# Attention and soft mixture of experts on one core: new order of all engines, new banks, second buffers for part of the transposed probabilities

## The chip, the cores and the metric

The kernel runs on one core of one Trainium2 chip. The time is the device time of one launch in microseconds (us), the median of the runs shown. TensorE does the matrix products and the transposes into PSUM, VectorE (DVE), ScalarE (ACT) and GpSimd (POOL) the rest, and SyncE (SP) issues the transfers between main memory and SBUF.

## The reference

q, k and v have 8 batches x 8 heads x 576 rows x 64 columns. The attention is masked by blocks of 64: a row sees its own block and those before it. Its output, 4608 rows of 512, goes through a soft mixture of experts with 8 experts of 4 slots each.

```python
scores = scale * np.matmul(q, k.transpose(0, 1, 3, 2))
scores = np.where(mask, scores, -1000000000.0)      # mask: block_i >= block_j
attn = softmax(scores, axis=-1)                     # with + 1e-09 under the sum
x = (attn @ v).transpose(0, 2, 1, 3).reshape(4608, 512)
logits = x @ phi                                    # 512 x 32 slots
d = softmax(logits, axis=0)                         # over all 4608 rows
slot_input = (d.T @ x).reshape(8, 4, 512)
slot_out[e] = np.maximum(slot_input[e] @ w1[e], 0.0) @ w2[e]   # w1: 512x1024, w2: 1024x512
out = softmax(logits, axis=1) @ slot_out            # 4608 x 512
```

## The kernel before

Heads are taken two by two: a pair m (0 to 31, four to a batch) holds one head in partitions 0 to 63 and one in 64 to 127. The nine blocks of 64 rows are grouped by how many key blocks they see. For each pair TensorE does these steps, under the names of the table `TM`:

- UA, UB, UC: the products q k. UA (`qk` with "7") gives the scores of the rows that see up to 512 columns, UB (`qkb`) those with 576 ("8") and the short ones ("3", "2", "1", "0"), UC (`qk` with "5") those with 384.
- g7, gc, gd, g5 (`tr`, line 501): the transposes of the normalized probabilities, 16, 10, 12 and 12 of them, into a pair of PSUM banks (`ptb`).
- pv0 and pv1 (`pv`, line 539) and pa (`pv8`, line 549): the products with v, which give the columns of x.

Between them VectorE takes the row maxima (rm, line 454) and the reciprocals of the sums (z, line 470), ScalarE the exponentials (ex, line 464), GpSimd normalizes (nm, line 481), adds epsilon (ze, line 474) and scales k (ks, line 373). The copies out of PSUM (eg7, og7, ..., for the two banks "e" and "o" of each group of transposes, xa and xb for the output of pa and pv) are done by ScalarE (line 339) or VectorE (line 341), as the table `EN` says.

For each batch the mixture of experts adds: prt0 to prt4 (logits, lines 568 and 579), their statistics (stats, stats1, stats2, lines 596 to 621) and `keep_l` (lines 626 and 627), which keeps the logits for the second softmax; ndt, the transposition of the exponentials; xq0, xq1 and xn4 (`xnat`, line 682), x transposed back, with copies en; sl and sl4, the products that collect the slots; sacc and sacc4, which add them up on VectorE. After the last batch mg0 to mg6 merge the running maxima, `formed` (line 730) builds the slots' input siT, and the experts follow: up (line 948), down (line 968), and the combination with the second softmax. `combine` for the first four batches ("comb0", "comb1") and `turn_c(0)`, a VectorE transposition, prepare that softmax.

The order of every engine is fixed by hand: each step is entered with `at(m * T + TM[...], ...)`, with T = 9.2, the steps are sorted by that number, and each engine runs its own in that order. Keys with ".0" to ".3" are for pair m mod 4, A to D for pairs 0 to 3, w and y for pairs 30 and 31, v and z for the last two batches. Below, "g7.23" is step g7 of pair 23, "xq1#6" step xq1 of batch 6.

Of SBUF, one big tile `arena` holds q, k, v, the probabilities and the transposed probabilities pt0 and pt1 (one buffer for each head); the areas that become free at the end take pieces of the experts' weights, 1 MB each. k is loaded into `kr` and scaled into `ks0` or `ks1` in turns. At the very start eight `warm` matmuls on zeros run before the first data, and two groups of `fill` matmuls later.

Of the kernel before, what the change touches and what calls it, by code (L numbers as in the profile page):

```python
# [29 lines left out]
PT1, PT8, PTN = 896, 1280, 1600  # L30
# [8 lines left out]
ONE = "82"  # L39
# [6 lines left out]
for name, n in (  # L46
    *((f"x{i}", S) for i in XIN), ("kr", S), ("q0", S), ("ks0", S), ("p7_0_0", 512), ("p7_1_0", 512),
    ("p5_0_0", 384), ("p5_1_0", 384),
    ("p3_0", 256), ("p1_0", 128), ("p0_0", 128), ("q1", S), ("ks1", S), ("p8", 640), ("v0", 640),
    ("p3_1", 256), ("p2", 256), ("p1_1", 128), ("p0_1", 128),  # L50
    *((f"p{t}_{j}_1", 64 * t + 64) for t in (7, 5) for j in range(2)),
    ("v1", 640), ("pt0", PTN), ("pt1", PTN), ("phi", 128),
):
    AREAS[name] = (LATE0, LATE0 + n)
    LATE0 += n
# [11 lines left out]
    "T": 9.2, "lkA": -5.94771, "lqA": -2.81305, "lkB": -10.95031, "lqB": -8.91013, "ksA": 2.22677, "UAA":  # L67
    2.24077, "rm71A": 2.24477, "rm70A": 2.24877, "ex71A": 2.25277, "ex70A": 2.25677, "lkC": -15.5701, "UBA":
    5.41282, "rm3A": 5.41482, "rm2A": 5.41682, "rm0A": 5.41882, "rm1A": 5.42082, "ex3A": 5.42282, "ex0A":
    5.42482, "ex1A": 5.42682, "ex2A": 5.42882, "lvB": 0.16944, "UCA": 10.43497, "lqC": -7.96303, "ksB": 4.13543,  # L70
# [134 lines left out]
def tile_attention_softmoe(  # L205
# [81 lines left out]
    with ExitStack() as c1:  # L287
# [15 lines left out]
        def endz(b):  # L303
            return "z" * (b == NB - 1)
# [738 lines left out]
```

## Time and profile before

| | us |
|---|---|
| median of 3 runs | 364.29 |
| range of the runs | 363.56 to 366.44 |
| profiled execution | 365.06 |
| its span, first to last instruction | 363.2 |
| TensorE busy | 347.2 (96%) |
| VectorE busy | 269.2 (74%) |
| ScalarE busy | 268.3 (74%) |
| GpSimd busy | 206.5 (57%) |

The profile is of one execution; times in it count from the first instruction. The attention fills the span to about 303 us, the rebuilding of the last batch to 311.6 us, the experts and the combination the rest. A matmul's busy time includes what it waits in the pipeline behind the one before it.

### The profile page before, as it was taken

Reading aid. Unit: us, or ns where it says so; the run is one execution under the profiler, and the core shown is the slowest. Engines: PE = TensorE matmul, PEld = TensorE weight load, DVE = VectorE, ACT = ScalarE, POOL = GpSimd, SP = SyncE. Lnnn points to the kernel's source line nnn. Section 1 sums busy time; section 2 is a strip of 40 time slices with the busy share of each in tenths; the row PEclk is TensorE's granted clock in tenths of the full one; section 3 lists DMA queues with packets and bytes.
Section 4 is the critical chain, followed back from the end, with each engine's and each line's share of the span. In section 5 each row is a group of like instructions: output and inputs, shape, how many; then the busy total and the mean of one; then the engine's idle time right before and its main releaser. Section 6 shows DMA issues by size and latency. Waiting matters only on the chain.

```text
span 363.2 us, 14376 instructions
## 1 busy us (share of the span) xinstructions
PE 347.2 (96%) x5724; PEld 237.3 (65%) x5724; DVE 269.2 (74%) x756; ACT 268.3 (74%) x855; POOL 206.5 (57%) x472
## 2 busy tenths in 40 slices
PE   8899999999999999999999999999999999999983
PEld 3666666777667766776777676767676766446641
DVE  4877767978897888778877887788778866463442
ACT  3877889887978798889888988898888776022341
POOL 3886577757766776676666666666667573000000
PEclk9999999999999999999999999999999999999995
DMA  6656363654473546453854473627413069999886
GB/s 202 213 192 210 99 175 139 222 168 143 139 279 116 167 147 212 131 189 88 255 189 133 154 240 111 208 68 248 128 45 119 19 229 378 389 423 422 346 347 279
DMA packets 29218, 72.29 MB, mean 199 GB/s; under 512 B 6880, under 2 KB 15200, under 8 KB 24160
## 3 DMA queue, kind: packets, MB, share of 16 engines
q1 hardware_dynamic: 29152, 71.38, 57.2%
q8 instruction: 45, 0.74, 0.8%
q14 instruction: 21, 0.17, 0.1%
HBM read 61.93 MB, written 9.44 MB: 196 GB/s over the span
## 4 chain that ended last, share of the span: by engine, by line
PE 60%; DVE 6%; ACT 1%; issue 1%; POOL 1%; DVEq 0%; ACTq 0%; POOLq 0%
PE x L539 13%; PE sc L412 10%; PE pt_e L501 9%; PE sc L433 5%; PE so L968 4%; PE x L549 4%; PE hp L948 4%; PE o L925 3%; DVE stat L454 2%; PE pt_o L501 2%; PE x L568 2%; DVE arena L341 2%; PE x L702 1%; PE x L682 1%; PE x L579 1%
## 5 line engine op out<-in xcount | busy, mean ns | idle before, releaser
L481 POOL TENSOR_SCALAR arena<-arena,stat 128x512 f32<-128x512 f32 (+6 forms) x288 | 153.1, 548 | 56.2 <-DVE stat L470 38.2
L464 ACT ACTIVATE arena<-sc,stat 128x512 f32<-128x512 f32 (+6 forms) x282 | 150.8, 547 | 9.1 <-DVE stat L454 7.7
L454 DVE TENSOR_REDUCE stat<-sc 128x1 f32<-128x512 f32 (+4 forms) x251 | 130.0, 545 | 8.4 <-PE sc L433 5.5
L501 PEld LDWEIGHTS pt_e<-ident,arena 64*128 64x128 f32 x789 | 60.9, 138 | 35.9 <-POOL arena L481 12.3
L501 PE MATMUL pt_e<-ident,arena 64*128 64x64 f32 x789 | 75.2, 229 | 5.4 <-DVE arena L341 2.3
L539 PE MATMUL x<-arena 128*64 128x128 f32 (+2 forms) x640 | 76.1, 384 | 0.2
L501 PE MATMUL pt_o<-ident,arena 64*128 64x64 f32 x789 | 74.8, 229 | 0.2
L412 PE MATMUL sc<-arena 64*128 64x512 f32 (+1 forms) x252 | 63.2, 583 | 0.2
L501 PEld LDWEIGHTS pt_o<-ident,arena 64*128 64x128 f32 x789 | 59.7, 138 | 3.2 <-ACT arena L339 2.1
L539 PEld LDWEIGHTS x<-arena 128*64 128x64 f32 x640 | 41.1, 136 | 30.2 <-issue 18.2
L464 ACT ACTIVATION_READ_ACCUMULATOR arena<-sc,stat 128x1 f32 x282 | 58.5, 208 | 0.0
L339 ACT COPY arena<-pt_o 128x384 f32<-128x384 f32 (+1 forms) x87 | 44.4, 511 | 16.5 <-PE pt_o L501 13.2
L341 DVE COPY arena<-pt_e 128x384 f32<-128x384 f32 (+2 forms) x72 | 40.9, 568 | 10.2 <-PE x L539 7.4
L433 PE MATMUL sc<-arena 64*64 64x192 f32 (+2 forms) x752 | 43.3, 341 | 0.3 <-ACT arena L464 0.3
L433 PEld LDWEIGHTS sc<-arena 64*64 64x64 f32 x752 | 36.2, 133 | 8.6 <-issue 3.2
L339 ACT COPY arena<-pt_e 128x384 f32<-128x384 f32 (+2 forms) x54 | 26.8, 495 | 16.6 <-PE pt_o L501 13.7
L474 POOL TENSOR_SCALAR stat<-stat 128x2 f32<-128x2 f32 (+1 forms) x96 | 18.9, 197 | 31.2 <-ACT arena L464 26.1
L470 DVE RECIPROCAL stat<-stat 128x2 f32<-128x2 f32 (+1 forms) x96 | 15.5, 167 | 24.7 <-POOL stat L474 23.7
L549 PE MATMUL x<-arena 128*64 128x64 f32 x640 | 25.7, 227 | 0.0
L373 POOL TENSOR_SCALAR arena<-arena 128x576 f32<-128x576 f32 x32 | 21.6, 675 | 6.1 <-DMA arena<-in_k 4.7
L549 PEld LDWEIGHTS x<-arena 128*64 128x64 f32 x640 | 21.3, 137 | 5.6 <-ACT xn L339 3.3
L341 DVE COPY arena<-pt_o 128x384 f32<-128x384 f32 (+2 forms) x39 | 20.6, 529 | 3.8 <-PE pt_o L501 1.7
(166 smaller groups left out, 362.2 us busy)
## 6 DMA issues: line engine op xcount, KB each, us to landing
arena<-in_w SPq DMA_DIRECT2D x32, 1024.0 KB, 7.2
arena<-in_k SPq DMA_DIRECT2D x32, 288.0 KB, 3.2
arena<-in_q SPq DMA_DIRECT2D x32, 288.0 KB, 3.1
arena<-in_v SPq DMA_DIRECT2D x32, 256.0 KB, 3.2
out<-arena SPq DMA_DIRECT2D x7, 1024.0 KB, 5.8
arena<-in_v SPq DMA_DIRECT2D x32, 32.0 KB, 3.1
out<-arena SPq DMA_DIRECT2D x2, 512.0 KB, 4.8
out<-arena SPq DMA_DIRECT2D x4, 256.0 KB, 3.9
```

The lines of the kernel that those rows point to most:

```text
L339: nc.scalar.copy(out=out, in_=in_)
L341: nc.vector.tensor_copy(out=out, in_=in_)
L373: nc.gpsimd.tensor_scalar(out=area(f"ks{m % NQB}"), in0=area("kr" if m > 1 else f"ks{m}"), scalar1=SCALE, scalar2=0.0, op0=ALU.mult, op1=A ...
L412: nc.tensor.matmul(scores(t + str(j), m), lhsT=q[r, lo:lo + 128], rhs=k[r, 0:NC[t]], start=True, stop=True)
L433: nc.tensor.matmul(o, lhsT=a, rhs=b, start=True, stop=True)
L454: nc.vector.tensor_reduce(out=st[:, 0, u:u + n], in_=sc, axis=AX.XY if x == "8" else AX.X, op=ALU.max, negate=True)
L464: nc.scalar.activation(out=pr, in_=sc, func=AF.Exp, bias=st[:, 0, u:u + 1], accum_out=st[:, 1, u:u + 1],)
L474: nc.gpsimd.tensor_scalar(out=st[:, 2, c], in0=st[:, 1, c], scalar1=EPS, scalar2=1.0, op0=ALU.add, op1=ALU.mult)
L481: nc.gpsimd.tensor_scalar(out=pr, in0=pr, scalar1=st[:, 2, u:u + 1], scalar2=0.0, op0=ALU.mult, op1=ALU.add)
L501: nc.tensor.transpose(out=trbank(m, g)[i][:, 64 * n:64 * n + 64], in_=prob(m, x)[r, 128 * c:128 * c + 128], identity=ident[r, r],)
L539: nc.tensor.matmul(xps[m, 0][64 * j:64 * j + 64, lo:hi], lhsT=vs(m)[:, j, c, :], rhs=rhs, start=a, stop=z, skip_group_check=True,)
L549: nc.tensor.matmul(xps[m, 1][64 * j:64 * j + 64, 0:64], lhsT=vs(m)[:, j, c, :], rhs=arena[:, lo:lo + 64], start=(c == 0), stop=(c == NQ - 1),)
```

## The change

k is loaded straight into `ks0` or `ks1` and scaled there. The transposed probabilities of g7 and g5 that pv reads now have two buffers, pa0 and pa1, used in turns; those of gd (pb) and gc (pc) have one. For that the probabilities "3", "0" and "5" have one buffer instead of two. PSUM is cut into four pairs of banks, and a table `BK` names the pair or bank of every step. Bank pair 3 has most transposes as before, but pair 0 puts gc and g5 into bank pair 0, pair 2 puts g5 there. `TM` and `EN` have new numbers for all steps. In the last batch several steps are split in two: the copy xb, part4, the statistics, the transposition ndt, the copies dn, xnat (three pairs, then the fourth), slots, and `formed`, whose halves are copied by ScalarE and by VectorE. `turn_c(0)` stands behind the first "turn" of the experts instead of ahead of them, and the first half of "comb0" and "comb1", comb0, stands in pair 24 instead of pair 31.

```diff
-ONE = "82"
+ONE = ("8", "2", "3", "0", "50", "51")
...
-    *((f"x{i}", S) for i in XIN), ("kr", S), ("q0", S), ("ks0", S), ("p7_0_0", 512), ("p7_1_0", 512),
-    ("p5_0_0", 384), ("p5_1_0", 384),
-    ("p3_0", 256), ("p1_0", 128), ("p0_0", 128), ("q1", S), ("ks1", S), ("p8", 640), ("v0", 640),
-    ("p3_1", 256), ("p2", 256), ("p1_1", 128), ("p0_1", 128),
-    *((f"p{t}_{j}_1", 64 * t + 64) for t in (7, 5) for j in range(2)),
-    ("v1", 640), ("pt0", PTN), ("pt1", PTN), ("phi", 128),
+    *((f"x{i}", S) for i in XIN), ("q0", S), ("ks0", S), ("p7_0_0", 512), ("p7_1_0", 512), ("p1_0", 128), ("v0", 640), ("pa0", PTA), ("q1", S), ("ks1", S), ("p8", 640), ("p3", 256), ("p2", 256), ("p1_1", 128), ("p0", 128),
+    ("p7_0_1", 512), ("p5_0", 384), ("p5_1", 384), ("p7_1_1", 512), ("pa1", PTA), ("v1", 640), ("pb", 2 * PTB), ("pc", 2 * PTC),
...
+BK = {
+    "S7.0": 1, "SB.0": 1, "S8.0": 2, "S5.0": 2, "Tg7.0": 3, "Tg5.0": 3, "Tgc.0": 3, "Tgd.0": 3, "PB.0": 0, "PA.0":
...
+    "PB.3": 0, "PA.3": 0, "S7A": 1, "SBA": 3, "S8A": 2, "S5A": 0, "Tg7A": 3, "Tg5A": 0, "TgcA": 0, "TgdA": 3, "PBA":
...
+    1, "PAA": 0, "S7B": 1, "SBB": 1, "S8B": 2, "S5B": 2, "Tg7B": 3, "Tg5B": 3, "TgcB": 3, "TgdB": 3, "PBB": 0,
+    "PAB": 0, "S7C": 1, "SBC": 1, "S8C": 2, "S5C": 2, "Tg7C": 3, "Tg5C": 0, "TgcC": 3, "TgdC": 3, "PBC": 1, "PAC":
...
-        xbk = [ps.tile([128, 512], F32, name=f"x{i}") for i in range(2)]
-
-
-
-        scm = [ps.tile([128, 512], F32, name=f"sc{j}") for j in range(2)]
-        scn = ps.tile([128, 1024], F32, name="sc8")
-
-        ptb = [ps.tile([128, 512], F32, name=f"pt_{x}") for x in "eo"]
-
-        def xbank(key, z=""):
-            return xbk[EN["X" + key + z]]
+        duo = [
+            ps.tile([128, 1024], F32, name=f"duo{i}") if i in WIDE else [ps.tile([128, 512], F32, name=f"one{i}{j}") for j in range(2)]
+            for i in range(4)
+        ]
...
+        def bank(key, z):
+            return BK.get(key + z, BK.get(key))
...
-            nc.sync.dma_start(out=area("kr" if m > 1 else f"ks{m}"), in_=kT[b, p])
+            nc.sync.dma_start(out=area(f"ks{m % NQB}"), in_=kT[b, p])
...
-                out=area(f"ks{m % NQB}"), in0=area("kr" if m > 1 else f"ks{m}"), scalar1=SCALE, scalar2=0.0, op0=ALU.mult, op1=ALU.add
+                out=area(f"ks{m % NQB}"), in0=area(f"ks{m % NQB}"), scalar1=SCALE, scalar2=0.0, op0=ALU.mult, op1=ALU.add
...
-            return scm if m == NB * NP - 1 and g in ("gc", "g5") else ptb
+            return two(bank("T" + g, sfx(m)))
...
-                dst = both[:, i, PT8:PTN]
+                dst = area("pc").rearrange("p (j c) -> p j c", j=2)[:, i]
             elif g == "gd":
-                dst = both[:, 1 - i, PT1:PT8]
+                dst = area("pb").rearrange("p (j c) -> p j c", j=2)[:, 1 - i]
             else:
                 lo = 64 * i + (0 if g == "g7" else 128)
-                dst = both[:, :, 0:256 * (n // 2)].rearrange("p j (c s) -> p j c s", s=256)[:, :, :, lo:lo + 64]
+                pa = AREAS[f"pa{m % 2}"][0]
+                dst = arena[:, pa:pa + 2048].rearrange("p (c j s) -> p j c s", j=2, s=256)[:, :, 0:n // 2, lo:lo + 64]
                 src = src.rearrange("p (j c s) -> p j c s", j=2, s=64)
             copy("eo"[i] + g, dst, src, late(m) or f".{m % NP}")
 
 
...
-                    lo = AREAS[f"pt{j}"][0]
-                    both = arena[:, lo:lo + 2 * PT1].rearrange("p (i c) -> p i c", i=2)[:, :, 0:256]
-                    todo = [(0, 0, 512, both), (1, 256, 384, pt[:, PT1 + 256:PT8])]
+                    both = arena[:, pa:pa + 2 * (pb - pa)].rearrange("p (i c) -> p i c", i=2)[:, :, 0:256]
+                    todo = [(0, 0, 512, both), (1, 256, 384, arena[:, pb + 256:pb + PTB])]
...
-        def part4(b):
-            for p in range(NP):
+        def part4(b, ps=range(NP)):
+            if b < NB - 1:
+                mo[b, "xl4"] = mo[b, "xlg"][:, 128:192]
+            elif ps[0] == 0:
+                mo[b, "xl4"] = one(BK["L4z"])[:, 0:64]
...
+        def stats(b, i):
+            if (b, "bm") not in mo:
+                mo[b, "bm"] = sm.tile([128, 6], F32, tag="bm", name=f"bm_{b}")
+            for j in range(2) if i == 2 else (i,):
+                nc.vector.tensor_reduce(
+                    out=mo[b, "bm"][:, j:j + 1], in_=logits(b, j), axis=AX.X, op=ALU.max, negate=True
+                )
...
+        def formed(b, h):
+            ps = mo["si", h] = one(BK[f"F{h}z"])
+            nc.tensor.matmul(ps[:, 0:64], lhsT=acc4, rhs=fident[:, 64 * h:64 * h + 64], start=True, stop=False)
+            for i in range(2):
+                c = 2 * h + i
                 nc.tensor.matmul(
-                    scm[1][:, NS * c:NS * (c + 1)], lhsT=acc[:, 128 * c:128 * (c + 1)], rhs=fstack, start=False, stop=(c == 3)
-                )
-
-        def copied(b):
-            nc.vector.tensor_copy(out=siT, in_=scm[1][:, 0:128].rearrange("p (c s) -> p c s", s=NS))
+                    ps[:, NS * i:NS * (i + 1)], lhsT=acc[:, 128 * c:128 * (c + 1)], rhs=fstack, start=False, stop=(i == 1)
+                )
+
+        def copied(b, h):
+            copy(f"ci{h}", siT[h], mo["si", h][:, 0:64].rearrange("p (c s) -> p c s", s=NS), "z")
...
+        miscz = {
+            **misc, "prt4": (part4, (0, 1, 2)), "prt4B": (part4, (3,)), "el4": (evac_l4,), "stats": (stats, 0),
+            "stats4": (stats, 1), "stats2": (stats2, 0), "stats24": (stats2, 1), "ebm": (stats2, 2), "enl": (keep_l, 0),
+            "enl4": (keep_l, 1), "ndt": (natural, 0), "ndt4": (natural, 1), "disp": (dispatch, 0), "disp4": (dispatch, 1),
+            "dispB": (dispatch, 2), "xq3": (xnat, 3), "en3a": (evac_n, 3, 0), "en3b": (evac_n, 3, 1),
+            "sl": (slots, 0), "slB": (slots, 1), "sacc": (slots_acc, 0), "saccB": (slots_acc, 1),
+            "siT": (formed, 0), "siTB": (formed, 1), "siC": (copied, 0), "siCB": (copied, 1),
+        }
...
-        turn_c(0)
...
             turn(qd, 0)
+            if qd == 0:
+                turn_c(0)
```

Of the tables the diff shows a line or two. What they move is seen in the order of the instructions. The first place is SyncE's queue at the start. Before (in_k is a load of k, in_q of q, in_v of v, which takes two):

```order
L356 DMA arena<-in_k 128x576
L352 DMA arena<-in_q 128x576
L356 DMA arena<-in_k 128x576
L352 DMA arena<-in_q 128x576
L356 DMA arena<-in_k 128x576
L363 DMA arena<-in_v 128x2x256
L367 DMA arena<-in_v 64x2x64
L800 DMA arena<-in_phi 128x128
```

And now:

```order
L391 DMA arena<-in_k 128x576
L398 DMA arena<-in_v 128x2x256
L402 DMA arena<-in_v 64x2x64
L387 DMA arena<-in_q 128x576
L391 DMA arena<-in_k 128x576
L387 DMA arena<-in_q 128x576
L884 DMA phi<-in_phi 128x128
```

Both loads of v of pair 0 now stand ahead of its q, and k of pair 2 comes later.

The second place is VectorE in the steady part, pairs 23 and 24. A reduction from sc_110 is the row maximum of "8", the reciprocal of two columns is z0.24, the copy from pt_e of 384 columns egd.23. Before:

```order
L454 TENSOR_REDUCE stat_113<-sc_110 128x1
L341 COPY arena<-pt_o 128x320
L454 TENSOR_REDUCE stat_113<-sc_109 128x1
L454 TENSOR_REDUCE stat_113<-sc_108 128x1 x2
L470 RECIPROCAL stat_113<-stat_113 128x2
L341 COPY arena<-pt_e 128x384
```

Now, where duo_111, one_109 and one_110 are the banks of the scores, one_107 that of pa, one_113 and one_112 those of the transposes, and the reduction of c_all is the first step of "comb0", which stands here and in no other batch:

```order
L507 RECIPROCAL stat_115<-stat_115 128x2
L286 TENSOR_REDUCE mx_4568<-c_all 128x18
L507 RECIPROCAL stat_114<-stat_114 128x2
L376 COPY arena<-one_107 128x64
L491 TENSOR_REDUCE stat_114<-duo_111 128x1
L376 COPY arena<-one_113 128x320
L491 TENSOR_REDUCE stat_114<-one_110 128x1
L491 TENSOR_REDUCE stat_114<-one_109 128x1 x2
L376 COPY arena<-one_112 128x384
```

The reciprocal z0.24 (the line just ahead of the copy from one_107) has moved from just before egd.23 to ahead of the row maximum of "8".

The third place is the end. TensorE around UC of pair 31, the matmul of 128x384. Before, with the last transposes of g5.30, then pv of pair 30, and g7.31:

```order
L501 MATMUL pt_o<-ident,arena 128x64
L412 MATMUL sc_110<-arena 128x384 x2
L539 MATMUL x_106<-arena 64x512 x2
L539 MATMUL x_106<-arena 64x128 x2
L539 MATMUL x_106<-arena 64x256 x4
L539 MATMUL x_106<-arena 64x128 x2
L501 MATMUL pt_e<-ident,arena 128x64
```

Now, with the last transposition of gd.30 before it and xq1 of batch 6 behind it:

```order
L538 MATMUL one_113<-ident,arena 128x64
L448 MATMUL duo_111<-arena 128x384 x2
L753 MATMUL one_107<-ident,xT_116 128x64
L753 MATMUL one_108<-ident,xT_116 128x64
L753 MATMUL one_107<-ident,xT_117 128x64
```

UC of pair 31 now comes ahead of xq1#6, pa.30 and the logits blocks prt0#7 and prt1#7, and g5.30 has moved to the head of this stretch. And VectorE after the last pv, from the maximum of the logits on. Before:

```order
L596 TENSOR_REDUCE bm_5335<-x_107 128x1
L597 TENSOR_REDUCE bm_5335<-x_107 128x1
L626 STREAM_TRANSPOSE c_all<-lt_5333 128x128
L627 STREAM_TRANSPOSE c_all<-lt_5333 64x32
L604 TENSOR_TENSOR mrun_91<-mrun_90,bm_5335 128x2
L605 TENSOR_TENSOR bm_5335<-mrun_91,mrun_90 128x2
```

Now:

```order
L649 TENSOR_REDUCE bm_5335<-one_112 128x1
L649 TENSOR_REDUCE bm_5335<-one_113 128x1
L657 TENSOR_TENSOR mrun_92<-mrun_91,bm_5335 128x2
L658 TENSOR_TENSOR bm_5335<-mrun_92,mrun_91 128x2
L376 COPY lt_5360<-one_113 128x64
L376 COPY xn<-one_110 128x2x3x64
```

The two transposes of c_all from lt have moved from between the maxima and the running minimum (mrun) to a place further back, and the logits' last quarter has a bank of its own (one_113).

## Rows read from the trace of the kernel before

**Rows 1.** The page's first part: busy time, share and instructions of each engine.

```profile
PE 347.2 (96%) x5724; PEld 237.3 (65%) x5724; DVE 269.2 (74%) x756; ACT 268.3 (74%) x855; POOL 206.5 (57%) x472
```

**Rows 2.** Stages: length, each engine's busy us (instructions), granted clock, DMA share, GB/s.

```profile
10.00:20.00 10.00, 8.94 (x136) 6.15 (x136) 8.92 (x28) 9.06 (x33) 8.44 (x20) 1.00 0.70 224
120.00:160.00 40.00, 39.60 (x663) 28.19 (x661) 32.08 (x94) 34.40 (x113) 27.45 (x63) 1.00 0.58 183
289.92:303.19 13.27, 12.76 (x214) 8.95 (x211) 8.22 (x23) 8.75 (x27) 8.38 (x18) 1.00 0.73 275
303.19:311.62 8.43, 7.55 (x141) 5.37 (x139) 7.10 (x24) 4.10 (x13) 2.28 (x6) 1.00 0.95 368
```

**Rows 3.** TensorE's waits over the span: us in total, times, longest.

```profile
PE pt_e L501 <- DVE arena L341: 2.3, 6, 0.4
PE pt_e L501 <- ACT arena L339: 1.6, 3, 0.6
```

**Rows 4.** SyncE's timeline at the start: start us, us, what.

```profile
3.06 0.65 SPq L363 DMA_DIRECT2D arena<-in_v  x1
3.76 0.60 SPq L367 DMA_DIRECT2D arena<-in_v  x1
```

**Rows 5.** Stages from UA to the next block: pair 0's UA, UB, pair 1's UA.

```profile
4.51:6.52 2.01, 2.01 (x5) 0.51 (x4) 0.00 (x0) 0.00 (x0) 1.28 (x6) 1.00 0.90 314
6.52:7.81 1.29, 1.29 (x26) 1.17 (x24) 1.11 (x4) 0.19 (x1) 0.00 (x0) 1.00 0.83 270
9.21:10.28 1.07, 1.07 (x7) 0.31 (x5) 0.82 (x2) 1.07 (x7) 0.99 (x3) 1.00 0.54 123
```

**Rows 6.** TensorE's timeline at gd of pair 0: start, us, what, [idle before].

```profile
15.41 0.24 PE L501 MATMUL pt_e<-ident,arena 64*128 64x64 f32 x1 [0.79 <-DVE stat L470]
```

**Rows 7.** Chain of waits from 210 to 220: start us, us, what.

```profile
210.69 0.50 PE x L682 x16
...
216.14 0.76 DVE stat L454
216.89 0.41 DVE arena L341
...
217.44 0.24 PE pt_e L501
```

**Rows 8.** VectorE's timeline in pair 23 to 24.

```profile
226.86 0.16 DVE L470 RECIPROCAL stat<-stat 128x2 f32<-128x2 f32 x1
227.01 0.56 DVE L341 COPY arena<-pt_e 128x384 f32<-128x384 f32 x1
```

**Rows 9.** The page's sixth part: DMA issues, KB each, us to landing.

```profile
arena<-in_w SPq DMA_DIRECT2D x32, 1024.0 KB, 7.2
arena<-in_k SPq DMA_DIRECT2D x32, 288.0 KB, 3.2
```

**Rows 10.** VectorE's timeline from 300 to 307.

```profile
300.30 0.74 DVE L262 TENSOR_REDUCE mx<-c_all 128x18 f32<-128x576 f32 x1
...
305.56 0.29 DVE L596 TENSOR_REDUCE bm<-x 128x1 f32<-128x128 f32 x1 [0.27 <-ACT lt L339]
...
305.90 0.30 DVE L626 STREAM_TRANSPOSE c_all<-lt 128x128 f32<-128x128 f32 x1
306.22 0.21 DVE L627 STREAM_TRANSPOSE c_all<-lt 64x32 f32<-64x32 f32 x1
```

**Rows 11.** Chain of waits in the last pair.

```profile
292.01 0.73 PE x L549 x20
292.75 0.57 PE x L568 x16
...
294.13 0.73 PE sc L412 x4
...
298.06 0.60 POOL arena L481
...
300.89 2.38 PE x L539 x20
```

More of the change, by code (lines that the diff above doesn't have):

```diff
@@ L611, in stats1, with stats2 @@
             nc.gpsimd.tensor_tensor(out=bm[:, 2:4], in0=new, in1=old, op=ALU.subtract)
-        def stats2(b):
+        def stats2(b, i):
             bm, new = mo[b, "bm"], mrun[b % 2]
-            lt = logits(b)
-            for i, (sl, o) in enumerate(((slice(0, 128), 0), (slice(128, 192), 64))):
-                nc.scalar.activation(
-                    out=dt[:, sl.start + o:sl.stop + o], in_=lt[:, sl], func=AF.Exp, bias=new[:, i:i + 1], accum_out=bm[:, 4 + i:5 + i]
-                )
-            nc.scalar.activation(out=bm[:, 2:4], in_=bm[:, 2:4], func=AF.Exp)
@@ L623, in keep_l @@
-        def keep_l(b):
+            for j in range(3) if i == 3 else (i,):
+                if j < 2:
+                    nc.scalar.activation(
+                        out=dt[:, 192 * j:192 * j + 128 - 64 * j], in_=logits(b, j), func=AF.Exp, bias=new[:, j:j + 1],
+                        accum_out=bm[:, 4 + j:5 + j],
+                    )
+                else:
+                    nc.scalar.activation(out=bm[:, 2:4], in_=bm[:, 2:4], func=AF.Exp)
+        def keep_l(b, i):
             lt, u, k = mo[b, "lt"], b // 4, b % 4
@@ L634, in dispatch, with natural @@
-        def dispatch(b):
+            if i != 1:
+                nc.vector.transpose(
+                    out=c_all[:, u, 4 * k:4 * k + 4, :].rearrange("p i s -> p (i s)"), in_=lt[:, 0:128]
+                )
+            if i:
+                nc.vector.transpose(out=c_all[r, u, 16 + k // 2, :], in_=lt[r, 128:160])
+        def natural(b, i):
+            if i == 1:
+                mo[b, "nat4"] = one(BK["D4z"])
+                nc.tensor.transpose(out=mo[b, "nat4"][:, 0:64], in_=dt[0:64, 128:256], identity=ident[0:64, 0:64])
+                return
+            mo[b, "nat"] = two(bank("ND", endz(b)))
+            for i, lo, o in ((0, 0, 0), (1, 0, 0), (0, 128, 64))[:3 if i else 2]:
+                r = slice(64 * i, 64 * i + 64)
+                nc.tensor.transpose(out=mo[b, "nat"][i][:, o:o + 64], in_=dt[r, lo:lo + 128], identity=ident[r, r])
@@ L694, in evac_n @@
-            copy(f"n{i if i < 2 else 4}{'ab'[h]}", dst, src, endz(b))
-        def slots(b):
-            p0 = xbank("si", endz(b)) if b != NB - 2 else scn[:, 0:512]
-            mo[b, "xsi"] = p0
-            w = DM if b < NB - 1 else DM // 2
-            for lo in range(0, DM, w):
-                for g in range(4):
-                    nc.tensor.matmul(
-                        p0[NS * g:NS * (g + 1), lo:lo + w], lhsT=dn[:, (0, 1, 3, 4)[g], :], rhs=xn[:, g, lo:lo + w],
-                        start=True, stop=True, tile_position=(0, NS * g),
-                    )
+            dst, n = xn.rearrange("q t (p g s) -> q t p g s", g=2, s=64), NP - (b == NB - 1)
@@ new lines, in evac_n, with slots @@
+            if i == 3:
+                dst, src = dst[:, :, NP - 1, h, :], bk[h][:, 0:64 * NQ].rearrange("q (t s) -> q t s", s=64)
+            elif i < 2:
+                dst, src = dst[:, 2 * i:2 * i + 2, 0:n, h, :], bk[h].rearrange("q (t p s) -> q t p s", t=2, s=64)[:, :, 0:n]
+            else:
+                dst, src = dst[:, 4, 0:n, h, :], bk[h][:, 0:64 * n].rearrange("q (p s) -> q p s", s=64)
+            copy(f"n{(0, 1, 4, 3)[i]}{'ab'[h]}", dst, src, endz(b))
+        def slots(b, h=0):
+            p0 = one(bank("SIJ"[0] + "IJ"[h], endz(b)))
+            mo[b, "xsi", h] = p0
+            w = DM if b < NB - 1 else DM // 2
+            lo = w * h
+            for g in range(4):
+                nc.tensor.matmul(
+                    p0[NS * g:NS * (g + 1), 0:w], lhsT=dn[:, (0, 1, 3, 4)[g], :], rhs=xn[:, g, lo:lo + w],
+                    start=True, stop=True, tile_position=(0, NS * g),
+                )
@@ L707, in slots4 @@
         def slots4(b):
-            p0 = xbank("si4") if b != NB - 2 else ptb[0][:, 256:384]
+            p0 = one(bank("S4", endz(b)))
             mo[b, "xsi4"] = p0
@@ L785, in tile_attention_softmoe @@
             at(tb + TM[f"mg{i}z"], merge, NB - 1, i)
[L786 to L787 removed]
         for k, n in FILL.items():
             if k[-1] == "z":
[L790 removed]
+                at(tb + TM[k] + 0.0005, fill, one(FZ), n)
             else:
```

254 lines of the change are left out of this document (137 added, 117 removed), and 240 rows, old and new, of tables (BK, EN, TM).

## Prediction

> **What bounds the kernel now.** I read the page's first part, then the busy times by stage, then the list of TensorE's waits, and last the timeline at the places that the change touches. TensorE is busy for 347.2 of 363.2 us [rows 1], so it sets the time, and 16.0 us in all are idle. By stage [rows 2] the fast pairs of the middle leave it 0.4 us in 40, the first pairs 1.06 in 10, the 13.27 us between the last "UB" and the end of the last pv 0.51, and the 8.43 us from there to the first expert matmul 0.88. Busy does not mean unhindered: a transpose whose bank is still being copied out counts as busy while the next one cannot follow, so the stalls are a little larger than the idle time. The waits [rows 3] are nearly all at line 501, the transposes of the probabilities, for a VectorE copy (2.3 us) or a ScalarE copy (1.6 us), and once for 0.79 us behind a reciprocal in VectorE's order [rows 6]. That is where new buffers and banks could help, and 4.7 us is their whole sum. VectorE, ScalarE and GpSimd are not the bound in the middle (32.1, 34.4 and 27.5 of 40 us [rows 2]); between 10 and 20 us ScalarE has 9.06 and VectorE 8.92 of 10, so there they nearly are.
>
> **The change, part by part.** The matrix work stays: TensorE's order from "UC" of pair 4 to "UB" of pair 31 is the old one but for the order of three logits blocks. So the sum has three places: the start, the middle, the end.
>
> *Start, later.* SyncE now issues both loads of v of pair 0 ahead of its q. They took 0.65 and 0.60 us to issue [rows 4], so q leaves SyncE 1.25 us later. Its place behind one load instead of none costs a bit less than that at the landing, because the loads share the engines; I take 1.1 us for the start of "UA" of pair 0. [...]
>
> [...]
>
> *Start, sooner.* In pairs 0, 1 and 2 "gd" waits for the copies of "gc", since all transposes share one pair of banks: the gap at 15.41 us is 0.79 us [rows 6], and the two other pairs show the same (three in all). Now gc of pair 0 has other banks than gd, and pv1 or g5 stand between gc and gd of pairs 1 and 2. Full return: 3 x 0.79 = 2.4 us; nothing, if the copies are what is late. ScalarE and VectorE are both about 90% busy here [rows 2], so what TensorE stops waiting for in one place it will mostly wait for in the next: I take a quarter, 0.6 us. Start: 0.4 - 0.6 = **-0.2 us**.
>
> *Middle.* The second buffer for g7 and g5 frees their copies from the pv of the pair before. It would pay if the copies' start were held by pv. The stall that recurs once a batch is another. VectorE ends xb only as "UB" ends, at 216.1, then does the row maximum of the 576-wide block (0.76 us) and the copy that empties gc's bank (0.41 us), and only at 217.44 does gd begin [rows 7]. TensorE has gc in between, ten transposes of some 0.04 us, and the sixteen of xq1, 0.50 us [rows 7]: it is ready at 217.0, and loses some 0.5 us a batch. The new order has xb, the row maximum and the copy in the same sequence, and gc and gd share a bank as before, so this stays. What goes: z0 (0.16 us) no longer stands just before the copy egd that g5 waits for [rows 8], worth 0.14 us in one pair of four, and a GpSimd normalization that gd of pair 1 of a batch waits for comes earlier, again 0.14 us. What comes: in the second pair z0 now stands behind another copy, which delays a normalization and g7 by some 0.15 us. Net -0.13 us a batch, in six batches **-0.8 us**. The bounds are the whole of the L501 waits, -4 us, and a new wait of a copy's length (the third rival).
>
> k scaled in place: a load of k must now wait until "UC" of two pairs before is done, where it waited for a GpSimd scaling. The load takes 3.2 us by its median, a w piece in its way 7.2 [rows 9], and the scaling well under 1 us comes after. From UC.(m-2) to UA.m it has one pair and more, over 9.2 us (the table's T): 5 us to spare, and straight behind a w piece about 1. SyncE's queue holds the next loads behind a waiting one, and q and v have as much time. Cost: nothing; 1 us a time if the cover is gone. The single buffers of p5, p3 and p0 let ScalarE's exponentials of pair m wait for transposes of pair m-1, which stand a row maximum and more ahead of them: nothing. The first half of the fold of c moves from pair 31 to pair 24: one 0.74 us reduction of VectorE [rows 10] amid its tight copies, **+0.2 us**; it ended under pv before. The transposition of c's first half, moved behind the first "turn", lay in the shadow of "formed" and lies in that of the expert matmuls: nothing either way.
>
> *End, before the last pv.* "UC" of pair 31 moves ahead of 16 transposes of batch 6 (0.50 us unhindered [rows 7]), pv8 (0.73) and two logits blocks (0.57). From UC at 294.13 the chain runs through a row maximum, exponentials and a normalization (0.60 us, to 298.66) to g5 and on to the last pv [rows 11], so it can start 1.8 us sooner. But TensorE has its work to do. Two pv of 2.4 us, two pv8 of 0.73, the logits (0.57 and a third of some 0.25), UC 0.73, xq1 0.50 and 87 other transposes of about 0.045 us (an estimate from the sixteen of [rows 7] at 0.03 and those of [rows 6] at 0.06 apart, 3.9 us) make 12.2 of the 13.27 us, and about as much after the change (a logits block out, 24 transposes in). So at most 1.1 to 1.7 us can come back, and I take **-1.05 us**, since gd of pair 30 now follows g5 of pair 30 into the same bank and must wait for its copies. Bounds 0 and -1.7.
>
> *End, after it.* The statistics no longer wait for ScalarE's copy of the logits (0.27 us), nor does the running minimum wait for the two transposes of keep_l (0.30 and 0.21 us), which now come later [rows 10]; slots and "formed" go in halves. But VectorE is busy 7.10 of the 8.43 us [rows 2], ScalarE has more small copies (xn for three pairs, then for the fourth), and every split adds an instruction of 0.2 us or so. Of the 0.78 us I keep **-0.45 us**; bounds -1.3 (formed's first half hidden as well) and +0.5 (the extra instructions lengthen the chain).
>
> Sum: -0.2 - 0.8 + 0.2 - 1.05 - 0.45 = -2.3 us. From the profiled execution, 365.06 us, that makes 362.76; the median of the runs is 0.77 below it, so **362.0 us**. The runs of before spread over 2.9 us, so 1% (3.6 us) is about what can be told from no change.
>
> **The rivals.**
>
> [...]
>
> *The banks pay in full.* The three gaps of the start come back (-1.8 more), and the end takes its far bounds (-0.6 and -0.85 more): 358.8. For it: the waits are for copies, and copies get new banks; against: the 90% of ScalarE and VectorE there.
>
> *VectorE's new order makes a new wait (slower than before).* VectorE does its work strictly in program order in every row that I read. z0 of the second pair of a batch now stands behind the copy ogd of the pair before (a copy like the 0.56 us of [rows 8]), which itself waits for a transposition of the pair before; GpSimd's normalization waits for z0, and g7 for that. By the middle's account it costs 0.15 us in one pair of four. If GpSimd is later than in the old trace, by its own new order, the whole copy shows: 0.56 us in that pair, +3.4 us in six batches less what is counted, 365.0 with the middle's gain lost as well 365.8, still no loss beyond the noise. It decides from two pairs of four on: 6.7 us, 368 to 369, slower. For it: every engine's order is new at once; against: GpSimd has 27.5 of 40 us to do.
>
> *The second buffers do nothing* is part of the forecast for the middle.
>
> **How the numbers follow.** The forecast, 361 to 364, 0.45; the clock, 363.4 to 365, 0.15; the banks in full, 358.4 to 361, 0.27; the new wait, 365 to 369, 0.13. The range leaves out half of the last and a tenth at the lower end: 358.8 to 366.2. Faster by over 1% (below 360.65) is most of the banks' case and a small part of the forecast's, 0.28; slower by over 1% (above 367.9) over half of the last, 0.08; within 1% the rest, 0.64.
>
> **What the changed kernel's profile would show.** [...] UC.4 starts near 43.5 (43.74 before). The same place of the steady pairs 36.7 us later in each batch, with the 0.5 us stall after VectorE's row maximum still there once a batch. The last pv ends some 2.1 us sooner counted from the span's start, and the first expert matmul follows 8.0 us after it, in place of 8.43. The rest of the span stays as long as it was, 51.6 us. The prediction is wrong if pairs 4 to 30 differ by over 1.5 us in all, or if the waits at the transposes vanish altogether.

## The result, and the profile after

The changed kernel takes 369.31 us (median of 4 runs, 368.61 to 371.34) against 364.06 for the kernel before: ratio 1.0136, 95% interval 1.0108 to 1.0163. It is 1.4% slower; 362.0, a little faster than before, was forecast, and 369.31 lies outside the stated 358.8 to 366.2.

The profiled execution took 371.34 us, its span 369.2 us, 6.0 more than before. The page's first part and its issues:

```profile
PE 348.8 (94%) x5726; PEld 239.4 (65%) x5726; DVE 274.4 (74%) x764; ACT 258.0 (70%) x853; POOL 205.2 (56%) x471
...
arena<-in_w SPq DMA_DIRECT2D x32, 1024.0 KB, 7.3
arena<-in_k SPq DMA_DIRECT2D x32, 288.0 KB, 2.9
arena<-in_q SPq DMA_DIRECT2D x32, 288.0 KB, 3.7
arena<-in_v SPq DMA_DIRECT2D x32, 256.0 KB, 4.2
```

TensorE is busy about as long as it was (348.8 us, 347.2 before [rows 1]); it is idle for 20.4 us in place of 16.0. q and the large load of v take longer to land (medians; 3.1 and 3.2 us before). The list of TensorE's waits (total, times, longest) says who made it idle:

```profile
PE one L584 <- DMA arena<-in_v: 2.7, 3, 1.8
PE one L538 <- DVE arena L376: 2.6, 6, 0.4
PE one L448 <- DMA arena<-in_q: 2.5, 1, 2.5
...
PE one L538 <- ACT arena L374: 0.9, 2, 0.6
PE one L584 <- issue: 0.7, 1, 0.7
PE one L538 <- POOL arena L518: 0.7, 1, 0.7
```

The waits at the transposes (line 538) add up to 4.2 us, 0.5 us less than before [rows 3], [rows 6]. Two waits for transfers are new: for q at UA (line 448) and for v at pv8, the step pa (line 584). Before, no TensorE wait in the list was for a transfer. Where the time went is best seen by when the same step starts in both traces (us, read off TensorE's timeline):

| step | before | after | difference |
|---|---|---|---|
| UA of pair 0 | 4.51 | 7.07 | +2.56 |
| UA of pair 4 | 35.96 | 39.33 | +3.37 |
| UA of pair 6 | 54.45 | 57.01 | +2.56 |
| UA of pair 17 | 155.24 | 158.21 | +2.97 |
| UA of pair 19 | 174.18 | 180.60 | +6.42 |
| UA of pair 26 | 238.35 | 245.80 | +7.45 |
| UB of pair 31 | 288.67 | 295.83 | +7.16 |
| end of the last pv | 303.19 | 308.99 | +5.80 |
| first expert matmul | 311.62 | 317.15 | +5.53 |

So the loss has three places: the first microseconds, pairs 17 and 18, and pieces of 0.6 and 1.0 us at pairs 8 and 24. Between them the pairs run a little faster than before, and the end is 1.63 us shorter. The experts and the combination take 52.05 us in place of 51.58.

The profiled execution is the longest of the four. The other three took 368.61 to 369.47 us at a mean granted clock of 0.988 to 0.991, where this one has 0.978; so these may have lost less by falls of the clock.

**The start.** SyncE's timeline, which answers to [rows 4], and the stages of UA, UB and UC of pair 0, which answer to [rows 5]:

```profile
0.73 0.39 SPq L391 DMA_DIRECT2D arena<-in_k  x1
1.18 0.66 SPq L398 DMA_DIRECT2D arena<-in_v  x1
1.89 0.59 SPq L402 DMA_DIRECT2D arena<-in_v  x1
2.52 0.59 SPq L387 DMA_DIRECT2D arena<-in_q  x1
```

```profile
7.07:8.13 1.06, 1.06 (x4) 0.30 (x4) 0.00 (x0) 0.00 (x0) 0.40 (x1) 1.00 0.44 156
8.13:10.45 2.32, 2.32 (x27) 2.03 (x25) 1.47 (x4) 1.26 (x4) 0.27 (x1) 0.52 0.00 1
10.45:11.86 1.41, 1.41 (x7) 0.50 (x5) 0.82 (x3) 0.88 (x5) 0.19 (x1) 0.58 0.00 0
160.00:200.00 40.00, 37.68 (x612) 26.50 (x609) 30.99 (x86) 29.70 (x101) 25.02 (x57) 0.96 0.50 169
```

q leaves SyncE at 2.52 us, 1.34 us later than before, about as forecast, but TensorE can start only at 7.07, not at 5.6 (4.51 us [rows 5] and the 1.1 us taken): q takes 4.41 us to land, where it took 3.15 before. UA itself takes 1.06 us, at a granted clock of 1.00. UB behind it does not run at that level: the granted clock is 0.52 and the block takes 2.32 us, where [rows 5] have 1.29 us. The clock had risen and fell again after the gap: the trace records the upper level, 1.0, from 4.80 us and the lower, 0.5, from 8.21 to 11.63. The 1.00 that [rows 5] print for UA of pair 0, which took 2.01 us, says nothing: the first clock record of that trace is the 1.0 from 6.66 us on, behind this block.

**Pair 16.** SyncE's timeline at 158 us, and TensorE at pv8 of that pair:

```profile
158.45 0.33 SPq L391 DMA_DIRECT2D arena<-in_k  x1
158.82 0.76 SPq L308 DMA_DIRECT2D arena<-in_w  x1
159.63 0.43 SPq L387 DMA_DIRECT2D arena<-in_q  x1
160.10 0.56 SPq L398 DMA_DIRECT2D arena<-in_v  x1
160.71 0.63 SPq L402 DMA_DIRECT2D arena<-in_v  x1
```

```profile
167.51 0.80 PE L584 MATMUL one<-arena 128*64 128x64 f32 x20 [1.85 <-DMA arena<-in_v]
```

The load of k of pair 18 goes out at 158.45, when UC of pair 16 has read the old k. Right behind it leave a w piece (1 MB of the experts' weights), q, and v of pair 16, whose pv8 TensorE could begin at 165.66. v arrives 1.85 us too late, and then the clock falls (0.5 from 168.64 to 172.05 us, 0.96 in the mean of the stage from 160 to 200 us, above). The us to landing of the piece and of v's large load:

```profile
arena<-in_w SPq DMA_DIRECT2D x1, 1024.0 KB, 7.3
...
arena<-in_v SPq DMA_DIRECT2D x1, 256.0 KB, 7.3
```

What decides how late v comes is the piece ahead of it. At pairs 8, 16 and 24 the piece took 5.8, 7.3 and 5.1 us, v landed 1.3 to 1.5 us behind it, and TensorE waited 0.60, 1.85 and 0 us; at pair 24 v was there just as pv8 was ready. In the kernel before, v had landed some 9 us ahead of pv8 in these pairs. The 1.0 us lost at pair 24 is thus no wait for v: the list has 0.7 us of it as "issue" (see the w piece later, below).

What SyncE itself waited for, most of its time at the load of k:

```profile
SPq L391 <- PE duo L448: 149.4, 27, 9.3
```

In the kernel before, no load of k waited for TensorE; they waited for GpSimd and for earlier loads, some 71 us in all.

### The profile page after: what moved, and what is told of

Same layout as the page of the kernel before. It is cut to its first block, busy times and chain, and to the rows that moved or that the text cites. A ratio compares the mean times of both kernels' runs of the same rounds, so it can differ in the third digit from the quotient of the medians.

```text
span 369.2 us, 14434 instructions
## 1 busy us (share of the span) xinstructions
PE 348.8 (94%) x5726; PEld 239.4 (65%) x5726; DVE 274.4 (74%) x764; ACT 258.0 (70%) x853; POOL 205.2 (56%) x471
## 4 chain that ended last, share of the span: by engine, by line
PE 69%; ACT 7%; DVE 7%; DMA 6%; POOL 3%; issue 3%; SPq 1%; DVEq 0%; POOLq 0%; ACTq 0%
PE one L574 14%; PE one L538 12%; PE one L448 6%; PE duo L448 5%; DMA arena<-in_v 5%; PE one L584 5%; ACT arena L501 5%; PE one L469 5%; PE so L1050 4%; PE hp L1030 4%; DVE stat L491 3%; PE o L1007 3%; PE duo L469 3%; POOL arena L518 2%; PE one L774 2%
## 5 line engine op out<-in xcount | busy, mean ns | idle before, releaser
L501 ACT ACTIVATE arena<-one,stat 128x512 f32<-128x512 f32 (+5 forms) x194 | 94.0, 499 | 11.0 <-DVE stat L491 10.8
L374 ACT COPY arena<-one 128x384 f32<-128x384 f32 (+3 forms) x136 | 62.7, 490 | 49.1 <-PE one L538 48.1
L538 PEld LDWEIGHTS one<-ident,arena 64*128 64x128 f32 x1588 | 64.8, 139 | 35.4 <-POOL stat L511 7.3
L376 DVE COPY arena<-one 128x384 f32<-128x384 f32 (+3 forms) x138 | 75.4, 563 | 11.9 <-PE one L538 10.4
L538 PE MATMUL one<-ident,arena 64*128 64x64 f32 x1588 | 75.9, 229 | 4.4 <-DVE arena L376 2.6
L491 DVE TENSOR_REDUCE stat<-one 128x1 f32<-128x512 f32 (+4 forms) x194 | 76.6, 435 | 1.9 <-PE one L469 0.8
L574 PE MATMUL one<-arena 128*64 128x256 f32 (+2 forms) x640 | 76.3, 384 | 0.0
L501 ACT ACTIVATE arena<-duo,stat 128x384 f32<-128x384 f32 (+1 forms) x94 | 59.5, 640 | 6.2 <-DVE stat L491 5.3
L574 PEld LDWEIGHTS one<-arena 128*64 128x64 f32 x640 | 40.9, 137 | 30.3 <-issue 19.0
L491 DVE TENSOR_REDUCE stat<-duo 128x1 f32<-128x576 f32 (+1 forms) x63 | 53.8, 853 | 9.1 <-PE duo L469 6.8
L584 PEld LDWEIGHTS one<-arena 128*64 128x64 f32 x640 | 21.5, 137 | 9.9 <-ACT xn L374 3.3
```

The lines of the kernel that those rows point to most:

```text
L374: nc.scalar.copy(out=out, in_=in_)
L376: nc.vector.tensor_copy(out=out, in_=in_)
L491: nc.vector.tensor_reduce(out=st[:, 0, u:u + n], in_=sc, axis=AX.XY if x == "8" else AX.X, op=ALU.max, negate=True)
L501: nc.scalar.activation(out=pr, in_=sc, func=AF.Exp, bias=st[:, 0, u:u + 1], accum_out=st[:, 1, u:u + 1],)
L538: nc.tensor.transpose(out=trbank(m, g)[i][:, 64 * n:64 * n + 64], in_=prob(m, x)[r, 128 * c:128 * c + 128], identity=ident[r, r],)
L574: nc.tensor.matmul(xps[m, 0][64 * j:64 * j + 64, lo:hi], lhsT=vs(m)[:, j, c, :], rhs=rhs, start=a, stop=z, skip_group_check=True,)
```

## The experiments

All are compared with the kernel before, run beside them (364.3 to 364.7 us).

**v ahead of k.** In one pair of four the load of v is issued ahead of the load of k of two pairs later.

```diff
-"lv.0": 20.568988
+"lv.0": 18.19
```

> The changed kernel, with the load of v of pairs 4, 8, 12, ... (one in four) issued just ahead of the load of k of two pairs later, in place of behind it, a w piece and a load of q. Queue theory: SyncE stands at that load of k until UC of two pairs before is done, because k is now scaled in the buffer it is loaded into, and v comes too late for pv8 of pairs 8, 16 and 24 (TensorE waits 0.6, 1.85 and 0.7 us there, and its clock falls after the second). Then the waits for v vanish from the list, and the time falls from 369.3 by 3 to 5 us to 364.3 to 366.3. Rival, sharing of the DMA engines: v is late because a w piece runs beside it; then the waits only move, and the time falls by less than 1.5 us. Rival, copies: pv8 waits for the copies of gc; then the time stays at 369.

Measured: 367.0 us (366.18 to 367.37), ratio 1.0065 [1.0041, 1.0089]. The waits for v are gone from the list. The gain of 2.3 us is below the stated 3 to 5; these were worked out from the changed kernel's profiled execution, its longest run, and the 0.7 us at pair 24 counted there was no wait for v. That the place of v in the queue costs the time is shown. Copies are out as the reason, since none was moved. Sharing is not: v now stands ahead of the w piece as well as ahead of k.

**q first.** Both loads of v of pair 0 go behind q and k of pairs 0 and 1.

```diff
-"lvA": -46.816983
+"lvA": -46.55
```

> The changed kernel, with both loads of v of pair 0 issued behind q and k of pairs 0 and 1, as in the kernel before. Start theory: q behind v costs 2.6 us at the first UA and, by the lower clock after that gap, 0.8 us more, of which 0.8 comes back by pair 6; UA of pair 0 starts near 4.5 us in place of 7.07, and the time falls by 2.5 to 3.3 us to 366.0 to 366.8. Rival: the start is bound by the copies of the first pairs, whose new order is worse; then UA of pair 0 starts at 4.5, but UA of pair 4 still near 38.5 to 39.3 and the time falls by less than 1 us.

Measured: 365.95 us (364.78 to 369.45), 1.0051 [1.0025, 1.0076], 3.4 us less than the changed kernel, a little more than stated. UA of pair 0 starts at 4.52, UA of pair 4 at 36.29. The start theory holds; the rival had UA of pair 4 at 38.5 or later.

Its trace shows one thing more. v stands where the changed kernel has it, and yet the waits of pairs 8 and 16 are missing from the list. The piece and v's large load at pair 16:

```profile
arena<-in_w SPq DMA_DIRECT2D x1, 1024.0 KB, 5.2
...
arena<-in_v SPq DMA_DIRECT2D x1, 256.0 KB, 5.4
```

With pieces of 5.0 to 5.2 us v lands just in time at pairs 8, 16 and 24, within 0.1 us or so of pv8. So this order leaves v no spare, and whether TensorE waits differs from execution to execution. The runs spread over 4.7 us, and the profiled one (364.81 us) is the second shortest.

**Both.**

> The changed kernel with both orders of loads mended (v ahead of k once in four pairs, q ahead of v in pair 0). If the two queue effects are all that went wrong, and the rest of the change does what the prediction's sum says for the middle and the end (-0.6 and -1.5 us), the time is 361 to 363 us, below that of the kernel before. If a third thing costs time, it is 364 or above, and the trace shows pairs 4 to 30 or the end longer than before.

Measured: 363.46 us (361.89 to 366.04), 0.9964 [0.9935, 0.9993]: a little below the kernel before, and between the two cases stated. v ahead is worth 2.5 us here and 2.3 without the mended start; q first is worth 3.5 us and 3.4. So two queue effects account for the loss, and one third thing is left, 0.7 us at pair 24:

```profile
236.78 0.33 PE L584 MATMUL one<-arena 128*64 128x64 f32 x2 [0.43 <-issue]
```

This row of the mended kernel is a gap inside pv8 that no engine and no load ended.

**k staged again.** The order of loads stays as changed, but k has its buffer of its own back; one w piece fewer is loaded during the attention.

```diff
-RES = 17
+RES = 16
...
-            nc.sync.dma_start(out=area(f"ks{m % NQB}"), in_=kT[b, p])
+            nc.sync.dma_start(out=area("kr" if m > 1 else f"ks{m}"), in_=kT[b, p])
```

> The changed kernel, order of loads as changed, but k is loaded into a buffer of its own and scaled from there, as before; for the room one w piece fewer is loaded during the attention (16 in place of 17). Queue theory: k's load no longer waits for UC, so SyncE is not held, v comes in time although it stands behind k and the piece; the waits for v vanish as in the run with v ahead, 364.3 to 366.5 us. Sharing theory: v still runs beside the w piece and stays late, 368 to 370. Copies theory: no change, 368 to 370.

Measured: 368.2 us (367.81 to 368.67), 1.0101 [1.0078, 1.0124]. By the time alone the queue theory would have failed. The list of waits shows that it did not:

```profile
PE one L448 <- DMA arena<-in_q: 3.0, 1, 3.0
PE one L538 <- DVE arena L376: 2.6, 6, 0.4
PE so L1050 <- issue: 1.4, 1, 1.4
```

No wait for v above 0.13 us is left, and from pair 4 on no pair loses anything: its UA starts are 4.83 us behind the kernel before at pair 4, 3.93 at pair 6, 3.62 at pairs 18 and 26, and 3.38 at pair 31. What hid the gain in this execution is the start, which went worse with the same loads in the same order (UA of pair 0 at 7.58, the clock up only at 13.0, UA of pair 4 4.83 us late against 3.37), and 0.8 us more of another wait (line 1050) in the experts.

That a wait is missing from one trace proves little here, as the run with q first shows. SyncE's rows at pair 16 show more:

```profile
154.18 0.43 SPq L308 DMA_DIRECT2D arena<-in_w  x1
159.15 0.33 SPq L387 DMA_DIRECT2D arena<-in_q  x1
159.53 0.79 SPq L398 DMA_DIRECT2D arena<-in_v  x1
```

The piece leaves 5.35 us ahead of v and has landed before v goes out; with k in place the two left within 1.28 us. pv8 of pairs 8, 16 and 24 has 2.9 to 3.3 us to spare, where it had none. So k scaled in place is what pushes the piece and v together just ahead of the step that needs v. Queue and sharing are not rivals here: the held queue makes v follow the piece at once, and the piece's time then sets the wait. Whether v is slowed by sharing the engines with the piece, or only by standing behind it, is not told apart.

**More warm matmuls.**

```diff
-WARM = 8
+WARM = 20
```

> The changed kernel with 20 warm matmuls ahead of the first UA in place of 8, so that TensorE has work while it waits for q. Clock theory: the gap of 2.5 us before UA of pair 0 makes the granted clock fall to 0.5 from 8.2 to 11.6 us, so that UB and UC of pair 0 take 2.31 and 1.41 us in place of 1.29 and 0.85; without the gap they run at the upper level and the time falls by 1 to 1.6 us to 367.7 to 368.3, UA of pair 0 still at about 7 us. Rival: the clock falls there for another reason, or the loss is made up by pair 6 anyway; then the time stays within 0.5 us of 369.3.

Measured: 366.4 us (365.56 to 369.64), 1.0073 [1.0044, 1.0102]. The stages of UA, UB and UC of pair 0:

```profile
7.46:8.52 1.06, 1.06 (x6) 0.30 (x5) 0.00 (x0) 0.00 (x0) 0.67 (x1) 1.00 0.30 103
8.52:9.77 1.25, 1.25 (x27) 1.12 (x25) 1.07 (x4) 0.16 (x1) 0.00 (x0) 1.00 0.00 0
9.77:10.62 0.85, 0.85 (x8) 0.30 (x5) 0.85 (x4) 0.85 (x3) 0.00 (x0) 1.00 0.00 0
```

UA starts even later, at 7.46, but the clock stays at 1.00 and UB and UC are short. By UA of pair 1 it is 1.24 us ahead of the changed kernel, as the clock theory has it. The medians differ by 2.9 us, more than the 1 to 1.6 stated, and the rest is not shown to come from the start: in its trace TensorE waits 0.11 us for v at pair 16, where the piece took 5.3 us, and 1.05 us at pair 24, where it took 6.3.

**In place in the old kernel, twice.** The first takes the staging buffer out of the kernel before and changes nothing else. In its order the loads of k of some pairs stand ahead of UC of two pairs before, so these UC read the wrong k and the output is wrong; only its time is of use. The second moves those loads behind UC.

```diff
-"lkC": -15.5701, "lkD": -11.23425, "lk.0": -4.67429, "lkw": -6.50068
+"lkC": -7.5, "lkD": -2.5, "lk.0": -1.0, "lkw": 1.0
```

> The kernel before with k loaded straight into the buffer where it is scaled, nothing else changed (the area of the staging buffer is unused). Theory: scaling in place costs only by what stands behind the load of k in SyncE's queue; in the old order that is seldom a load that is needed soon (v of pairs 8, 16, 24 stands ahead of the w piece and of k), so the time stays at 363.5 to 365.3. Rival: the wait for UC is too late by itself, k arrives late for UA; then TensorE waits at line 412 for the scaling and the time rises by 2 us and more.

> The kernel before with k loaded straight into the buffer where it is scaled, and the loads of k that stood ahead of UC of two pairs before (pairs 2, 3, 30 and one in four of the others) moved just behind it in SyncE's order, so that the output is right. Theory: in place costs only by what stands behind the load of k, and here v of pairs 8, 16 and 24 is ahead of it; k itself now stands behind a w piece in pairs like 12 and 20, with a whole pair of time. 363.5 to 366, no wait at pv8 for v. Rival: the wait for UC makes k itself late in every fourth pair, waits at line 412 or 433 of 0.5 us and more each, 367 and above.

Measured: 383.49 (381.74 to 385.25) and 382.07 us (381.03 to 384.95), ratios 1.0517 [1.0485, 1.0549] and 1.0493 [1.0443, 1.0544]. Both theories fail. The rivals had the sign, and k itself is late, but in the second run TensorE hardly waits for the scaling (0.2 us at line 412). The one that waits is GpSimd:

```profile
POOL arena L373 <- DMA arena<-in_k: 35.9, 17, 4.2
POOL arena L481 <- DVE stat L470: 24.0, 42, 3.1
```

In the old order the scaling of k stands early in GpSimd's row; k now comes later, GpSimd stands at it for 35.9 us (4.7 us in the kernel before), and normalizations queue behind it. In the changed kernel GpSimd waits 4.3 us for k. The new order of GpSimd is a likely reason, but no run tells it apart from the new places of the loads.

**One buffer for g7 and g5**, on the mended kernel: `pa1` in place of `pa0` and `pa1` in turns.

> The changed kernel with both orders of loads mended, but with one buffer in place of two for the transposed probabilities of g7 and g5. The prediction's step says that the second buffers give the middle nothing, since copies are held by the row maximum and the order of VectorE and not by pv: then the time is that of the mended kernel, 363.5, within 1 us. Rival: the new order rests on them; the copies of g7 then wait for pv of the pair before, and the time rises by 0.3 us a pair or more, to 370 and above.

Measured: 410.92 us (408.11 to 412.49), 1.1259 [1.1221, 1.1298]. The rival's sign, and far more than it asked:

```profile
PE one L574 <- DVE arena L376: 21.9, 13, 2.5
PE one L469 <- ACT arena L501: 7.3, 7, 1.2
PE one L574 <- ACT arena L374: 3.4, 2, 2.4
```

pv (line 574) waits for copies, which wait for the pv before (15.4 us of VectorE's waits). It is no proof that second buffers gain against the old order, which never had them; but the new order can't do without.

**The w piece later**, on the mended kernel: the piece that runs beside pair 24 is issued some 9 us later.

```diff
-            at((4 + 3.2 * i) / 2 * T, load_piece, i, arena[:, o:o + PIECE])
+            at((4 + 3.2 * i) / 2 * T + (8.0 if i == 15 else 0.0), load_piece, i, arena[:, o:o + PIECE])
```

> The changed kernel with both orders of loads mended, and the w piece that runs at 229 to 234 us in the mended kernel issued some 9 us later. Theory of fetching: the gap of 0.43 us at pv8 of pair 24, which the list of waits puts down to issue, is TensorE waiting for its instructions, whose 16 KB block is read at 234.39 us, just after that piece landed (234.14); in the kernel before the same block was read at 232.11. Then that gap goes and the block from pv8 to UC takes 0.73 us in place of 1.49: 0.4 to 0.8 us less, 362.7 to 363.1. Rival: the gap is a wait for a copy or for v that the list does not show; then the piece's place changes nothing there.

Measured: 362.86 us (360.97 to 363.09), 0.9942 [0.9921, 0.9963], the lowest median, though its interval overlaps that of the mended kernel. The gap at pair 24 is gone:

```profile
235.41 0.80 PE L584 MATMUL one<-arena 128*64 128x64 f32 x20
236.14 0.59 PE L448 MATMUL duo<-arena 64*128 64x384 f32 x2
```

**gc's copy ahead of the row maximum**, on that version, in one pair of four.

```diff
-"rm8.3": 11.447059
+"rm8.3": 11.6
```

> The mended kernel with the w piece moved, and in one pair of four VectorE does the copy that empties gc's bank ahead of the 576-wide row maximum, not behind it. The prediction's step for the middle says that gd waits 0.5 us a batch because of that order. Then the wait falls to 0.2 to 0.3 us and the time by 1.2 to 2 us, to 361 to 361.7 (mended: 362.86). Rival: the row maximum is what the next exponentials and UC wait for; then gd comes sooner, but UC or g5 later, and the time stays within 0.5 us or grows.

Measured: 366.5 us (364.97 to 368.0), 1.0052 [1.0033, 1.0072], 3.6 us worse. The rival is right. At pair 22 gd begins 1.20 us after gc in place of 1.50, and its wait is gone; but UC of pair 23 behind it begins 0.74 us later, since it waits for the exponential of the 576-wide block. The list has seven such waits:

```profile
PE duo L448 <- ACT arena L501: 5.5, 7, 0.9
```

## Why the prediction was wrong, point by point

The step that failed is the one on k scaled in place: "5 us to spare, and straight behind a w piece about 1", "q and v have as much time. Cost: nothing". It counted the time of k's own load and was right for k: no wait for k is in the list. It did not follow the loads behind it in the queue, which it named. v of pair 16 stood behind the load of k of pair 18, a w piece and a load of q, and had no time to spare: UC of pair 16, for which SyncE stood, is followed some 7 us later by pv8 of the same pair, which needs that v, and the piece takes 5.0 to 7.3 us ahead of it. The wait is 0.60 us at pair 8, 1.85 us at pair 16, and the granted clock of 0.5 from 168.64 to 172.05 us adds to it; from UA of pair 17 to UA of pair 19 the trace loses 3.45 us. Put at nothing, the term is 2.3 to 2.5 us in the medians, shown by v ahead with either start. That the hold by k is behind it is shown by k staged (2.9 to 3.3 us to spare in the unchanged order). The prediction's own sign of being wrong came true: from UA of pair 4 to UB of pair 31 the two traces differ by 3.79 us, over the 1.5 it allowed.

The second step that failed is the start. The 0.4 us by which the sum has it later is shown by no run; what the runs show in its place is the 3.4 us that q first gives back, with UA of pair 0 starting 2.56 us later and UB behind it 1.03 us longer in the changed kernel's trace. The 1.1 us for the start of UA were these 2.56: q not only left 1.3 us later but took 1.3 us longer to land, issued fourth in place of second. What it shared the engines with is not taken apart by a run. The issue times were all that the step used.

The clock was not to be forecast from one trace: with the same eight warm matmuls the first rise is at 6.66 us before, at 4.80 in the changed kernel and at 13.00 with k staged. The case of the clock, 363.4 to 365 us, had 0.15, and the clock did cost time at the start. In the changed kernel the level rose at 4.80 us, UA took 1.06 us, and then it fell: UB and UC have 0.52 and 0.58. In the trace with k staged, where it rose only at 13.00, UA of pair 0 took 2.01 us. UB of pair 0 took 2.32 us behind a gap of 2.49 us, and 1.25 us at a granted clock of 1.00 where 20 warm matmuls stood ahead of UA. So in these two traces the fall goes with the gap; by what rule the clock is granted is not shown.

The banks' gain at the start, taken as a quarter: with the loads mended and the piece moved, UA of pair 6 starts 0.59 us sooner than before. The sum had 0.6 for it. The size is right, the way to it less so: the three gaps are 0.79, 0.5 and 0.5 us, not three of 0.79, so their full return is 1.8 us and not 2.4. In the mended kernel all three are gone, and waits for GpSimd (0.7 us) and ScalarE (0.5 us) have come in their place, as the step expected of engines that are nearly full (ScalarE and VectorE are both busy for 9.19 of 10 us there).

The middle: forecast -0.8 + 0.2; from UA of pair 6 to UA of pair 31 the mended kernel with the piece moved gains 0.45 us. Right, within what can be read. The stall at gd stays as forecast, 0.4 us six times (line 538 for VectorE's copy, in the first list of waits):

```profile
222.72 0.75 DVE stat L491
223.47 0.41 DVE arena L376
223.87 0.14 issue
224.01 0.58 PE one L538 x12
```

These are the rows of the changed kernel's chain that answer to [rows 7]. What the step did not say, the last run shows: the order that makes gd wait is the better one. "The second buffers do nothing" is half wrong: no run shows them to give time against the old kernel, but the new order rests on them.

The end: forecast -1.05 before the last pv's end and -0.45 after it. Measured, 13.27 to 11.91 us (-1.36) and 8.43 to 8.16 us (-0.27), -1.63 in place of -1.50. VectorE there, for [rows 10]:

```profile
310.36 0.29 DVE L649 TENSOR_REDUCE bm<-one 128x1 f32<-128x128 f32 x1 [0.53 <-PE one L605]
310.81 0.23 DVE L649 TENSOR_REDUCE bm<-one 128x1 f32<-128x64 f32 x1 [0.15 <-PE one L620]
311.06 0.16 DVE L657 TENSOR_TENSOR mrun<-mrun,bm 128x2 f32<-128x2 f32 x1
```

The maxima now wait for TensorE's logits alone, and the running minimum follows the second of them at once.

So all the terms but two held. Without the later start, which the mended kernel does not have, they add up to -2.7 us. With the piece moved its span is 2.7 us below the old one in the profiled executions, and 1.8 us below in the medians; so near a hit is in part luck. The slower rival that was named (a new wait in VectorE's order) is in no trace; its sum is also off, since 0.56 us less the counted 0.15 makes 2.5 us in six batches and 364.5, not 365.0.

## What to carry to other kernels

When a load is made to wait for a consumer, list everything behind it in the same queue, and for each of these the step that needs it: the load that waits may have time where the ones behind it have none. Here the places of two loads cost 5.85 us, more than the rest of the change gained. An order that leaves a load no spare can show no wait in one execution and 1.85 us in the next, so read the time to spare and not only the list of waits. And a stage's start should be costed with all loads that run beside it: a load that left 1.3 us later arrived 2.6 us later, and UB and UC behind the late UA ran at granted clocks of 0.52 and 0.58 (2.32 and 1.41 us, against 1.25 and 0.85 with more warm matmuls).

## What the runs showed of the hardware that was not expected

- TensorE's granted clock fell twice after a gap that had ended before the fall: in the changed kernel UA ran at a level of 1.0 from 7.07, behind 2.49 us of idling, and 0.5 is recorded from 8.21 to 11.63 us. The same happened after the wait of 1.85 us at pair 16: TensorE worked from 167.51 on, and the level was 0.5 from 168.64 to 172.05.
- A gap of TensorE that the profile calls "issue" went with the reads of a queue that the page lists as instruction (q8: 45 reads, 0.74 MB, so 16 KB each). In the mended kernel one was read at 234.39 us, 11.7 us after the one ahead of it, just as a w piece had landed (234.14 us), and the gap of 0.43 us inside pv8 followed. With the piece moved the block was read at 232.26 us, 9.3 us after the one ahead, and the gap was gone. Four traces have this gap, always behind the 18th of pv8's 20 matmuls, with reads 11.4 to 12.3 us after the one ahead; in the changed kernel's the read is at 241.87 us, 11.9 us after the one ahead, and TensorE goes on at 244.17 us. The gap ends 2.3 to 2.4 us after the read of that block began, whether it is 0.14, 0.43, 0.69 or 1.10 us long; in three others of this order, with 9.3 to 10.3 us, there is none. That TensorE waits there for the instructions of that block, and that the piece held up the read, is inferred from these times.
